# A fused attention and two-MLP kernel: the PSUM homes of the up and down products exchanged, and weight differences made early

## Chip, core and metric

The kernel runs on one core of a Trainium2 chip. The metric is the device time of one execution in microseconds (us); lower is better. Three runs of the kernel before are known.

## What is computed

Three stages follow each other on 2304 tokens (4 batches of 576), all in fp32:

```python
scores = scale * q @ k.T + (cum[:, None] - cum[None, :]), causal     # cum: cumsum of log f
x = softmax(scores) @ v                        # (2304, 512)
h = x @ w_in                                   # first MLP, 1024 wide
ln = layer_norm(h * softmax(h)) * g_ln
x = ln @ w_out                                 # (2304, 512)
h = maximum(x @ w2_in, 0)                      # second MLP, 2048 wide
out = (h * h) @ w2_out                         # (2304, 512)
```

## The kernel before

**Order of the work.** Every step (one instruction, or a few of one kind) is added to a plan with its costs per engine, a due time, the keys that it reads and writes, and the PSUM slot that it takes. The planner `Plan.lay` places all steps by list scheduling; the instructions are then issued in the order of the planned starts, so each engine and the DMA queue of SyncE (SP) works through a fixed list in that order. A step that gets more work or another due time moves its neighbours too. The planner knows PSUM by keys (`z0`, `z1`, `xo`, `h`, and slots of `pp` and `hp`). What an instruction really waits for is settled by the tile that it touches. `Z[0]`, `Z[1]`, `XO` and the three `PP` are tiles of one PSUM bank each; `HP` is one tile of two banks:

```python
    Z = [ps.tile([P, 512], F32, name=f"z{i}") for i in range(2)]
    HP = ps.tile([P, 2, 512], F32, name="hp")
    PP = [ps.tile([P, 512], F32, name=f"pp{i}") for i in range(3)]
```

**Arithmetic.** Each fp32 operand is split into a high and a low part (`halves`: a copy, line 345, 349 or 351, and a subtraction, line 1087); a product is three matmuls (low by high, high by low, high by high).

**Stages.** Attention and the first MLP run interleaved until about 480 us: scores in `z` (line 536), exp on ACT (571), transposes in `pp` (590), the product with v in `xo` (610), the first MLP's `h` in `hp` (826 to 828), its layer norm on all engines (the last scaling on POOL is line 887, the transposes that follow line 903), and `ln @ w_out` in `pp` (777 to 779). Meanwhile `early2` brings w2_in and w2_out, which arrive as words that need a conversion, through five slots of the tile `free` to DRAM; one addition on POOL for each piece is line 703. w2_out goes to `w2d` as it is. For w2_in also the differences and sums that are needed later are made here and stored in `w2u`, split into both halves.

**The second MLP** works on nine blocks of 256 tokens and eight pairs `p` of 128-row pieces of the 2048 wide hidden layer.

- `half_up` (line 1284) makes the hidden layer of block 0 for each pair with 24 matmuls; then ACT does relu in place (1248) and square to SBUF (1253). Pairs 0 and 1 use `pp`, pairs 2 to 7 the two banks of `hp`.
- `unit` (line 1334) makes it for two blocks at once for a pair, with seven products (of six matmuls) instead of eight; ACT and DVE add them up (lines 345, 1348), then relu and square (1248, 1366, 1253). Units with an even number use `hp`, odd ones two slots of `pp`.
- `step` (lines 1420 to 1422) makes the down product of one block and one pair, again seven products, each of three matmuls, in two groups of 9 and 12. DVE forms the operands (1392) and they are split. The products of a block add up over the eight pairs in `z0`, `z1`, `xo` and one slot of `pp` (`m7`); at the block's end a copy (345) and seven additions (1437) fold them into the output. The last block uses `hp` and `pp`.
- `weights2` loads the w2_out pieces of a pair from `w2d`, forms four differences on DVE (line 1151, 32 in all) and splits the results. `weightsh` does the like for the half step. Both go through six raw buffers.

Of the kernel before, what the change touches and what calls it, by code (L numbers as in the profile page):

```python
# [8 lines left out]
F32 = mybir.dt.float32  # L9
# [231 lines left out]
def tile_kernel(ctx: ExitStack, tc: tile.TileContext, q, k, v, f, w_in, w_out, g_ln, w2_in, w2_out, out):  # L241
# [6 lines left out]
    P = 128  # L248
# [25 lines left out]
    w2d = dram.tile([KF2, 2, P, 512], F32, name="w2d")  # L274
    w2u = dram.tile([KF2 // 2, 7, P, 512], F32, name="w2u")
    sb = ctx.enter_context(tc.tile_pool(name="sb", bufs=1))
# [52 lines left out]
    pl = Plan(dict(pp=3, hp=2, rq=NRQ), ("z0", "z1", "xo", "h"))  # L329
# [338 lines left out]
    def convert(src, raw, w, hi, lo, n, prio, rawk, wk, outk, gain=None, to=None):  # L668


        def words():
            dst = raw().bitcast(U32)
            if len(src.shape) == 3:
                dst = dst.rearrange("p (c x) -> p c x", x=src.shape[2])
            nc.sync.dma_start(dst, src)

        def L():
            return raw().rearrange("p (n t) -> p n t", t=2)[:, :, 0]

# [34 lines left out]
        pl.add(dict(pool=tt), a5, prio, [lk], [wk])  # L714
        if to is not None:
# [288 lines left out]
    small += GS[5:] + GA[6:]  # L1004
# [18 lines left out]
    def early2():  # L1023
# [12 lines left out]
        def unit(n, fc, c, hf, prio):  # L1036
            i = n % 5
            convert(
                source2(fc, 2 * c + hf), lambda: both(i), lambda: place(i, 2), None, None, 256,
                prio, ("fr", i), ("fw", i), ("w2d", fc, c, hf), to=w2d[fc, c, :, hf * 256 : hf * 256 + 256],  # L1040
            )
            return i

        def part2(i, p, k, prio):
# [9 lines left out]
            pl.add(dict(dma=1140), lambda: nc.sync.dma_start(w2u[p, k], both(i)), prio, [lk, hk], [("w2u", p, k)])  # L1054
# [7 lines left out]

        n = 0
        for fc in range(KF2):
            for hf in range(2):
                unit(n, fc, 1, hf, EARLY0 + n * EARLYP)
                n += 1
        for p in range(KP):
# [4 lines left out]
            for i, k in ((a11, 0), (a12, 4), (a22, 5)):  # L1073
                part2(i, p, k, prio)
# [4 lines left out]
            for i, k in ((a21, 2), (a22, 3), (a11, 1), (a12, 6)):  # L1079
                part2(i, p, k, prio)  # L1080
# [19 lines left out]
    def load2(fc, c, prio):  # L1100
        ri = turn[0] % len(RAW)
        turn[0] += 1
        once(("raw", ri), RAW[ri], rk2(ri), prio)
        pl.add(
            dict(dma=1140), lambda: nc.sync.dma_start(RAW[ri][0](), w2d[fc, c]), prio - AHEAD,
            [("w2d", fc, c, z) for z in (0, 1)], rk2(ri),
        )
        return ri
# [24 lines left out]
    def weights2(p, prio):  # L1133
        W = W2[p]
        rr = [load2(2 * p + i, 1, prio) for i in range(2)]

        def place(nm, n):
# [4 lines left out]
        def split(nm, raw, rk, n):  # L1142
            halves(raw, rk, W[nm + "h"][0], ("w2", p, nm + "h"), W[nm + "l"][0], ("w2", p, nm + "l"), n, prio)

        a, b = slice(0, 256), slice(256, 512)
        r = [[lambda i=i, z=z: RAW[rr[i]][0]()[:, z] for z in (a, b)] for i in range(2)]
        k = [rk2(rr[0]), rk2(rr[1])]

        def diff(dst, x, y, rk, wk):
            def fn():  # L1150
                nc.vector.tensor_tensor(out=dst(), in0=x(), in1=y(), op=ALU.subtract)

            pl.add(dict(dve=335), fn, prio, rk, wk, port=True)

        place("a", 256)
        place("b", 512)
        place("s", 512)
        place("t", 512)
# [66 lines left out]
    last8 = [("hp", "l0"), ("hp", "l1"), ("pp", "l2"), ("pp", "l3")]  # L1225

    def bank(blk, i):
        if blk == NTB - 1:
            return last8[(i + 1) // 2 if i == 6 else i // 2]
        return m7 if i == 6 else ("z0", "z1", "xo")[i // 2]  # L1230

    def psum(k):
        if k[0] == "hp":
            return HP[:, pl.slot[k]]
        if k[0] == "pp":
            return at(k)
        return Z[0] if k == "z0" else Z[1] if k == "z1" else XO.rearrange("p c x -> p (c x)")
# [32 lines left out]
    def half_up(p, prio):  # L1270
        uid[0] += 1
        ck = ("pp" if p < HPP else "hp", uid[0])
        if p == HPP:
            pl.add(dict(dve=0), lambda: None, prio - 5000, [], ["h", "hp"])
        W = H2[p]
        for y, c in ((0, 0), (0, 1), (1, 0), (1, 1)):
            def up(y=y, c=c):
# [10 lines left out]

            rk = [("w2", p, f"u{c}{a}") for a in "hl"] + [("xo", 5 + y, a) for a in range(2)] + ["hp"] * (p >= HPP)
            pl.add(  # L1290
                dict(pe=6 * 116), up, prio, rk, [ck] + ["turn"] * (y + c == 0), take=None if y + c else ck,
                uses=[ck] if y + c else [],
            )
# [6 lines left out]
    def unit(b, p, prio):  # L1300
        n = (b - 1) * KP + p
        pool = "pp" if n % 2 else "hp"
        uid[0] += 2
        ks = [(pool, uid[0] - 1), (pool, uid[0])]
        lastks[pool] = ks
# [12 lines left out]
        def prod(i, prio):  # L1318
            m = (7 * n + i) % NU
            sk = ("us", m)  # L1320
            if sk not in first_use:
                once(sk, again(upper[m]), [sk], prio)
            pl.add(
                dict(dma=1140), lambda: nc.sync.dma_start(upper[m][0]().bitcast(F32), w2u[p, i]), prio - UAHEAD,
# [3 lines left out]
            def fn():  # L1328
# [13 lines left out]
                dict(pe=6 * 116), fn, prio, [sk, ("xo", i, 0), ("xo", i, 1), "hp"], [k] + ["turn"] * (i == 0),  # L1342
                take=k if opens_ else None, uses=[] if opens_ else [k],
            )

        def add(dst, x, i, prio, rk, wk, uses=(), take=None):
# [4 lines left out]
            pl.add(dict(dve=344), fn, prio, [k] + rk, wk, uses=[k] + list(uses), take=take)  # L1351
# [3 lines left out]
        copy(TB, u2f, lambda: half(0), prio, [ks[0]], [uk], [ks[0]])  # L1355
# [6 lines left out]
        for i in (4, 5, 6):  # L1362
# [4 lines left out]
            uses=[k], take=r1,  # L1367
# [8 lines left out]
    def step(blk, p, prio):  # L1376
# [275 lines left out]
HPP = 2  # L1652
# [53 lines left out]
```

## Time and profile before

| what | value |
|---|---|
| median of 3 runs (lowest, highest) | 864.44 us (863.93, 867.23) |
| the profiled execution | 866.17 us |
| its span from the first to the last instruction | 864.4 us |
| PE busy | 805.0 us (93%) |
| weight loads of PE (PEld) busy | 729.0 us (84%) |
| DVE, ACT, POOL busy | 646.6, 543.2, 369.8 us |
| mean granted TensorE clock | 0.984 of full speed |
| DMA | 151.52 MB, 175 GB/s |

Matmuls are pipelined: a matmul of 256 columns is shown with some 0.28 us, while the next starts 0.12 us after it. So a busy PE is not PE at its peak. Idle time before an instruction is put down to the instruction that released it. A number on an instruction's line is the line of the kernel before.

### The profile page before, as it was taken

How to read it: one execution, taken by the hardware profiler on the slowest of the kernel's cores; microseconds unless marked ns; L12 is line 12 of the kernel's file. 1: busy time of each engine (PE TensorE's matmuls, PEld its weight loads, DVE VectorE, ACT ScalarE, POOL GpSimd, SP SyncE). 2: the span in 40 equal slices, each digit the busy share in tenths (PEclk: the TensorE clock that was granted, in tenths of full speed). 3: DMA queues.
4: the chain of work that ended last, by engine and by line, in shares of the span. 5: the costliest groups of instructions: out<-in, count | busy, mean ns of one | idle time of the engine just before them, and what ended most of it. 6: DMA issues, size and time to landing. Idle time of an engine off the chain costs nothing.

```text
span 864.4 us, 18663 instructions
## 1 busy us (share of the span) xinstructions
PE 805.0 (93%) x6392; PEld 729.0 (84%) x6392; DVE 646.6 (75%) x1655; ACT 543.2 (63%) x1383; POOL 369.8 (43%) x528
## 2 busy tenths in 40 slices
PE   4878899999999999999999888999999999999997
PEld 2556687888888888888989788999999999999997
DVE  8797867887767766866658769888678767876777
ACT  6899977988687887887857555454324433533332
POOL 6468767665587767687753010010111121112110
PEclk9999889999999999999999999999999999999999
DMA  6643336655555555645556666484757676665501
GB/s 208 191 146 116 115 94 205 199 175 171 166 165 177 177 154 167 208 160 166 177 191 205 190 205 243 154 279 144 241 178 237 188 229 205 198 207 172 158 1 49
DMA packets 99869, 151.52 MB, mean 175 GB/s; under 512 B 12128, under 2 KB 41824, under 8 KB 99776
## 3 DMA queue, kind: packets, MB, share of 16 engines
q1 hardware_dynamic: 99776, 150.35, 55.0%
q8 instruction: 50, 0.82, 0.4%
q14 instruction: 43, 0.35, 0.1%
HBM read 117.58 MB, written 32.65 MB: 174 GB/s over the span
## 4 chain that ended last, share of the span: by engine, by line
PE 73%; ACT 11%; DVE 11%; issue 3%; POOL 1%; DVEq 0%; ACTq 0%; POOLq 0%
PE hp L1334 9%; PE pp L1334 9%; PE pp L590 5%; PE z L536 5%; PE xo L610 4%; PE z L1420 3%; PE z L1421 3%; PE pp L777 3%; PE z L1422 3%; PE hp L826 3%; PE pp L779 3%; PE pp L778 3%; ACT adj L571 3%; PE hp L828 3%; PE hp L827 3%
## 5 line engine op out<-in xcount | busy, mean ns | idle before, releaser
L536 PE MATMUL z<-k,q 80*64 80x288 f32 (+17 forms) x384 | 95.8, 348 | 11.9 <-DVE q L501 8.2
L571 ACT ACTIVATE adj<-z,st 64x288 f32<-64x288 f32 (+9 forms) x192 | 95.3, 499 | 17.2 <-DVE st L557 15.2
L590 PE MATMUL pp<-ident,adj 128*128 128x128 f32 (+1 forms) x480 | 82.4, 282 | 16.9 <-ACT adj L571 15.2
L590 PEld LDWEIGHTS pp<-ident,adj 128*128 128x128 f32 (+1 forms) x480 | 52.8, 145 | 43.3 <-ACT adj L571 28.5
L557 DVE CUSTOM_DVE_ANT_0 z<-z,maskb 128x128 f32<-128x128 f32 (+8 forms) x144 | 65.4, 464 | 29.6 <-PE z L536 25.7
L777 PE MATMUL pp<-ln,woh 128*128 128x256 f32 x288 | 84.8, 294 | 2.2 <-DVE ln L906 1.5
L345 ACT COPY pt<-pp 128x256 f32<-128x256 f32 (+5 forms) x167 | 68.1, 418 | 24.3 <-PE pp L590 23.2
L779 PE MATMUL pp<-ln,woh 128*128 128x256 f32 x288 | 81.7, 284 | 0.0
L778 PE MATMUL pp<-ln,wol 128*128 128x256 f32 x288 | 81.7, 284 | 0.0
L1087 DVE TENSOR_TENSOR k<-adj,k 128x512 fp32r<-128x512 f32 x75 | 52.4, 700 | 38.2 <-POOL k L349 26.3
L349 POOL TENSOR_SCALAR k<-adj 128x512 fp32r<-128x512 f32 x39 | 24.2, 620 | 124.2 <-DVE adj L1392 50.7
L536 PEld LDWEIGHTS z<-k,q 128*128 128x128 f32 (+3 forms) x384 | 58.7, 189 | 20.0 <-ACT pt L1526 8.2
L703 POOL TENSOR_TENSOR free<-free 128x256 uint32<-128x256 uint32 x64 | 50.8, 799 | 47.5 <-DVE free L697 42.8
L610 PE MATMUL xo<-pt,vn 128*64 128x128 f32 (+1 forms) x960 | 64.9, 277 | 0.4 <-ACT pt L345 0.3
L826 PE MATMUL hp<-wih,xl 128*128 128x512 f32 x144 | 62.6, 435 | 1.1 <-ACT hp L865 1.1
L349 POOL TENSOR_SCALAR ln<-q 128x384 fp32r<-128x384 f32 x29 | 15.5, 534 | 111.6 <-PE z L1422 42.5
L610 PEld LDWEIGHTS xo<-pt,vn 128*64 128x64 f32 x960 | 51.5, 143 | 11.6 <-issue 6.8
L777 PEld LDWEIGHTS pp<-ln,woh 128*128 128x128 f32 x288 | 55.5, 193 | 4.8 <-DVE ln L906 2.0
L827 PE MATMUL hp<-wil,xh 128*128 128x512 f32 x144 | 57.5, 399 | 0.2 <-DVE wil L707 0.2
L828 PE MATMUL hp<-wih,xh 128*128 128x512 f32 x144 | 57.4, 399 | 0.0
L778 PEld LDWEIGHTS pp<-ln,wol 128*128 128x128 f32 x288 | 55.9, 194 | 0.6
L779 PEld LDWEIGHTS pp<-ln,woh 128*128 128x128 f32 x288 | 55.9, 194 | 0.0
(594 smaller groups left out, 2619.3 us busy)
## 6 DMA issues: line engine op xcount, KB each, us to landing
ln<-w2u SPq DMA_DIRECT2D x119, 256.0 KB
k<-w2u SPq DMA_DIRECT2D x105, 256.0 KB
w2u<-free SPq DMA_DIRECT2D x56, 256.0 KB
kn<-in_k_dram SPq DMA_DIRECT2D x32, 256.0 KB
free<-in_moe_w_out_dram SPq DMA_DIRECT2D x32, 256.0 KB
w2d<-free SPq DMA_DIRECT2D x64, 128.0 KB
free<-in_moe_w_in_dram SPq DMA_DIRECT2D x32, 256.0 KB
vn<-in_v_dram SPq DMA_DIRECT2D x20, 256.0 KB
```

The costliest lines, as they stand in the source:

```text
L345: nc.scalar.copy(dst(), src())
L536: nc.tensor.matmul(dst, lhsT=ql[0:r, p, 0:m], rhs=rhs, start=(g == 0), stop=(g == 1))
L571: nc.scalar.activation(out=adj[0:m, c[1] : c[2]], in_=Z[c[0]][0:m, 0 : c[2] - c[1]], func=AF.Exp, bias=st[0:m, low : low + 1], scale=-1.0, ...
L590: nc.tensor.transpose(at(sk)[:, (c - g) * m : (c - g + 1) * m], adj[0:m, zc : zc + P], ident[0:m, 0:m])
L610: nc.tensor.matmul(XO[own[j], g // 2, off : off + m], lhsT=VN[vslot[b, c]][:, (g + j) * D : (g + j + 1) * D], rhs=PT[(s - h + g + j) % NPT ...
L777: nc.tensor.matmul(px, lhsT=woh[:, fc, w], rhs=lo, start=(fc == 0), stop=False)
L778: nc.tensor.matmul(px, lhsT=wol[:, fc, w], rhs=hi, start=False, stop=False)
L779: nc.tensor.matmul(px, lhsT=woh[:, fc, w], rhs=hi, start=False, stop=(fc == KF - 1))
L826: nc.tensor.matmul(HP[:, c], lhsT=XL[i][:, cc, :], rhs=wih[:, cc, w], start=(cc == 0), stop=False)
L827: nc.tensor.matmul(HP[:, c], lhsT=XH[i][:, cc, :], rhs=wil[:, cc, w], start=False, stop=False)
L828: nc.tensor.matmul(HP[:, c], lhsT=XH[i][:, cc, :], rhs=wih[:, cc, w], start=False, stop=(cc == KC - 1))
L1334: nc.tensor.matmul(half(i), lhsT=l, rhs=r[:, x], start=(i in (0, 2) and c + k == 0), stop=(c + k == 3), skip_group_check=True,)
```

## The change

1. The products of `half_up` and of even units go to `z0` and `z1` instead of `hp` (pairs 0 and 1 of the half step too, which used `pp`); the down products that were in `z0` and `z1` go to the two banks of `hp` (keys `h0`, `h1`). In the last block they go to `z0`, `z1` and two slots of `pp`.
2. `early2` makes the differences of w2_out too and stores the seven pieces of each pair in `w2f`; for the last pair it stores both halves, in `w2s`. `weights2` loads them and only splits them; for the last pair it loads both halves to their places.
3. `XOP[0]`, the split token operand of the first product, moves from the space of w_out (`woh`) to that of the low layer norm (`ln1`); weights get the space in exchange. The planner's cost of a load becomes 900 from 1140.

```diff
-    w2d = dram.tile([KF2, 2, P, 512], F32, name="w2d")
+    w2d = dram.tile([KF2, P, 512], F32, name="w2d")
+    w2f = dram.tile([KF2 // 2 - NPRE, 7, P, 256], F32, name="w2f")
+    w2s = dram.tile([NPRE, 7, P, 512], F32, name="w2s")
...
-    c = carve("woh", [512] * 8)
-    large += c[:6]
-    XOP = c[6:] + carve("wol", [512] * 8) + [carve(f"vn{i}", [512])[0] for i in range(4)]
-    XOP = [XOP[2 * j : 2 * j + 2] for j in range(7)]
+    c = carve("woh", [512] * 7 + [256] * 2)
+    large += c[:7]
+    small += c[7:]
+    XOP = carve("wol", [512] * 8) + [carve(f"vn{i}", [512])[0] for i in range(4)]
+    XOP = [None] + [XOP[2 * j : 2 * j + 2] for j in range(6)]
...
-    GA = carve("ln1", [384] * 4 + [512] * 2 + [256] * 2)
+    GA = carve("ln1", [384] * 4 + [512] * 3)
     upper += GA[4:5]
-    large += GA[5:6]
+    XOP[0] = GA[5:7]
...
+        def keep(i, p, k, prio):
+            if p >= KP - NPRE:
+                part2(i, w2s[p + NPRE - KP, k], ("w2s", p, k), prio)
+            else:
+                pl.add(dict(dma=570), lambda: nc.sync.dma_start(w2f[p, k], place(i, 2)), prio, [("fw", i)], [("w2f", p, k)])
...
+            for i, k in ((r00, 0), (r10, 1), (r11, 2)):
+                keep(i, p, k, prio)
+            add2(r00, r01, r00, ALU.subtract, prio)
+            add2(r01, r11, r01, ALU.subtract, prio)
+            for i, k in ((r00, 3), (r01, 4)):
+                keep(i, p, k, prio)
+            add2(r11, r11, r00, ALU.subtract, prio)
+            add2(r10, r11, r10, ALU.subtract, prio)
+            for i, k in ((r10, 5), (r11, 6)):
+                keep(i, p, k, prio)
...
-        rr = [load2(2 * p + i, 1, prio) for i in range(2)]
...
-        split("a", r[0][0], k[0][0:1], 256)
-        diff(r[0][0], r[0][1], r[0][0], k[0][1:], k[0][0:1])
-        split("b", RAW[rr[1]][0], k[1], 512)
-        diff(r[0][1], r[1][1], r[0][1], k[1][1:], k[0][1:])
-        split("s", RAW[rr[0]][0], k[0], 512)
-        diff(r[1][1], r[1][1], r[0][0], k[0][0:1], k[1][1:])
-        diff(r[1][0], r[1][1], r[1][0], k[1][1:], k[1][0:1])
-        split("t", RAW[rr[1]][0], k[1], 512)
+        for nm, n in (("a", 256), ("b", 512), ("s", 512), ("t", 512)):
...
+            if p < KP - NPRE:
+                src = w2f[p, c[0]] if n == 256 else w2f[p, c[0] : c[0] + 2].rearrange("c p x -> p c x")
+                ri = load2(src, [("w2f", p, k) for k in c], n, prio)
+                halves(
...
-    last8 = [("hp", "l0"), ("hp", "l1"), ("pp", "l2"), ("pp", "l3")]
+    last8 = ["z0", "z1", ("pp", "l2"), ("pp", "l3")]
...
-        return m7 if i == 6 else ("z0", "z1", "xo")[i // 2]
+        return m7 if i == 6 else ("h0", "h1", "xo")[i // 2]
...
-        ck = ("pp" if p < HPP else "hp", uid[0])
+        ck = f"z{p % 2}"
...
-        pool = "pp" if n % 2 else "hp"
-        ks = [(pool, uid[0] - 1), (pool, uid[0])]
+        ks = [("pp", uid[0] - 1), ("pp", uid[0])] if n % 2 else ["z0", "z1"]
...
-HPP = 2
+NPRE, LOAD2 = 1, 900
```

How the order of the instructions moves, at three places. On PE in the half step, where a pair follows another (`hp`, or `z_120` and `z_121`, is the bank written; the second name is the weight; bracketed: the engines on which a row waits). Before:

```order
L1284 MATMUL hp<-vn_49_5089,k_49_5248 128x256 [waits Activation_49]
L1284 MATMUL hp<-vn_49_5041,k_49_5248 128x256 x2
L1284 MATMUL hp<-vn_49_5089,k_49_5248 128x256
L1284 MATMUL hp<-vn_49_5044,k_49_5248 128x256 [waits Activation_49]
L1284 MATMUL hp<-vn_49_4211,k_49_5248 128x256 x2
```

The change, at the beginning of a pair in `z1` and of the next in `z0`:

```order
L1300 MATMUL z_121<-vn_49_5106,k_49_5371 128x256 [waits Activation_49]
L1300 MATMUL z_121<-vn_49_5079,k_49_5371 128x256 [waits DVE_49]
L1300 MATMUL z_121<-vn_49_5079,k_49_5371 128x256 x2
L1300 MATMUL z_121<-vn_49_5074,k_49_5371 128x256
L1300 MATMUL z_120<-vn_49_5106,pt_5503 128x256 [waits Activation_49]
```

Before, a pair waits for ACT twice, after its 6th and its 12th matmul; in the change once, at its first, and the other wait is for the split of its weights.

On PE around the transposes of the last layer norm (`e` is its input), the end of the matmuls ahead of them and of those behind. Before:

```order
L1284 MATMUL hp<-vn_49_5041,wil_5221 128x256 x2
L903 MATMUL pp_123<-ident_99,e_90 128x128 x4
L903 MATMUL pp_124<-ident_99,e_90 128x128 x4
L1284 MATMUL hp<-vn_49_5089,k_49_5175 128x256
L777 MATMUL pp_123<-ln_49_668,woh_74 128x256
```

The change:

```order
L1300 MATMUL z_121<-vn_49_4494,wil_5257 128x256 x2
L907 MATMUL pp_126<-ident_101,e_92 128x128 x4
L907 MATMUL pp_125<-ident_101,e_92 128x128 x4
L1300 MATMUL z_120<-vn_49_5106,wil_5257 128x256
L781 MATMUL pp_126<-ln_49_670,woh_76 128x256
```

Between the last matmul of `x @ w_in` and these transposes stood 30 matmuls of `ln @ w_out` and 78 of the half step; now 42 and 48. Behind them 18 of the half step still come ahead of the last 96 of `ln @ w_out`.

On PE where the first down product begins. Before:

```order
L1334 MATMUL hp<-woh_5577,k_49_5097 128x256 x6
L1334 MATMUL hp<-wol_5589,k_49_5097 128x256 x18
L1334 MATMUL pp_124<-wol_5589,ln_49_5635 128x256 x12
L1420 MATMUL z_118<-free_5324,ln_49_5579 128x256
L1421 MATMUL z_118<-k_49_5097,ln_49_5579 128x256
```

The change:

```order
L1300 MATMUL z_121<-vn_49_4494,e_5570 128x256 x2
L1434 MATMUL hp<-free_5561,ln_49_5597 128x256
L1435 MATMUL hp<-woh_5573,ln_49_5597 128x256
L1434 MATMUL xo<-wih_5427,k_49_5022 128x256
L1346 MATMUL z_120<-ln_49_5597,k_49_5115 128x256 x6
```

Before, 66 matmuls of units stood between the half step and the first down product; now it follows at once, with 30 matmuls, and the units come behind. From the second block on, the two orders agree but for the names of the banks.

## Rows read from the trace of the kernel before

**Rows 1.** Windows: span, PE, PEld, DVE, ACT, POOL busy (instructions), clock, DMA share, GB/s.

```profile
120.00:455.00 335.00, 328.65 (x2667) 282.88 (x2666) 242.04 (x649) 266.37 (x761) 230.78 (x327) 0.99 0.56 175
...
482.00:512.00 30.00, 23.29 (x166) 21.49 (x166) 18.37 (x36) 13.76 (x29) 3.38 (x6) 0.94 0.54 169
512.00:864.40 352.40, 334.94 (x2790) 330.00 (x2788) 267.88 (x704) 140.23 (x284) 48.28 (x83) 1.00 0.57 182
```

**Rows 2.** Waits of PE from 455 us on: total us, times, longest.

```profile
PE hp L1334 <- DVE xw L1348: 3.5, 4, 1.0
PE hp L1334 <- ACT xw L345: 3.2, 6, 0.9
PE hp L1334 <- ACT q L1366: 3.2, 6, 0.7
PE hp L1284 <- ACT q L1253: 2.2, 3, 0.7
PE hp L1284 <- ACT hp L1248: 2.2, 3, 0.8
PE hp L1334 <- issue: 1.5, 1, 1.5
PE hp L1334 <- ACT adj L1366: 0.9, 2, 0.5
PE hp L1334 <- ACT xh L1366: 0.9, 2, 0.5
PE pp L1420 <- DVE k L1087: 0.7, 1, 0.7
PE z L1420 <- DVE ln L1087: 0.6, 1, 0.6
PE hp L1334 <- ACT qn L1366: 0.5, 1, 0.5
PE hp L1284 <- ACT adj L1253: 0.4, 1, 0.4
```

**Rows 3.** Timeline of PE, 470 to 530 us: start, us, instructions, idle before.

```profile
481.94 3.74 PE L1284 MATMUL hp<-vn,k 128*128 128x256 f32 x30
...
486.35 0.98 PE L1284 MATMUL hp<-vn,k 128*128 128x256 f32 x6 [0.67 <-ACT hp L1248]
...
488.07 1.69 PE L1284 MATMUL hp<-vn,k 128*128 128x256 f32 x12 [0.75 <-ACT q L1253]
...
489.60 0.88 PE L1284 MATMUL hp<-vn,pt 128*128 128x256 f32 x6
...
497.86 1.55 PE L1284 MATMUL hp<-vn,pt 128*128 128x256 f32 x6 [0.75 <-ACT q L1253]
```

**Rows 4.** Timeline of ACT, 481 to 512 us.

```profile
485.71 0.58 ACT L1248 ACTIVATE hp<-hp 128x512 f32<-128x512 f32 x1 [0.54 <-PE hp L1284]
487.42 0.60 ACT L1253 ACTIVATE q<-hp 128x512 f32<-128x512 f32 x1 [1.13 <-PE hp L1284]
```

**Rows 5.** Groups of PE by line from 440 us on: busy, mean ns, idle before.

```profile
L1334 PE MATMUL pp<-wol,ln 128*128 128x256 f32 x234 | 31.1, 279 | 0.0
```

**Rows 6.** Timelines of PE and POOL around the last layer norm.

```profile
454.27 0.40 PE L828 MATMUL hp<-wih,xh 128*128 128x512 f32 x1
...
464.24 1.84 POOL L887 TENSOR_SCALAR e<-e,sm 128x1024 f32<-128x1024 f32 x1
...
467.32 1.04 PE L903 MATMUL pp<-ident,e 128*128 128x128 f32 x8
```

**Rows 7.** Timelines of DVE and PE at the end of block 0.

```profile
556.93 0.75 DVE L1437 TENSOR_TENSOR kn<-x,z 128x256 f32<-128x256 f32 x2
...
557.96 0.28 PE L1420 MATMUL z<-free,ln 128*128 128x256 f32 x1
```

**Rows 8.** Lines L703 and L1151: ns of one (least/median/most), first and last start.

```profile
L703 POOL TENSOR_TENSOR free<-free x64: 727/746/1200, 104.6 to 432.9; 128x256 uint32<-128x256 uint32 x64
...
L1151 DVE TENSOR_TENSOR kn<-kn x8: 419/426/717, 464.7 to 528.3; 128x256 f32<-128x256 f32 x8
```

More of the change, by code (lines that the diff above doesn't have):

```diff
@@ L328, in tile_kernel @@
     NU, NRQ = 13, 11
-    pl = Plan(dict(pp=3, hp=2, rq=NRQ), ("z0", "z1", "xo", "h"))
+    pl = Plan(dict(pp=3, hp=2, rq=NRQ), ("z0", "z1", "xo", "h", "h0", "h1"))
     uid = [0]
@@ L714, in convert @@
         pl.add(dict(pool=tt), a5, prio, [lk], [wk])
+        if to is False:
+            return
         if to is not None:
@@ L983, in tile_kernel @@
     more("free", 7, 1)
-    c = carve("woh", [512] * 8)
-    large += c[:6]
-    XOP = c[6:] + carve("wol", [512] * 8) + [carve(f"vn{i}", [512])[0] for i in range(4)]
-    XOP = [XOP[2 * j : 2 * j + 2] for j in range(7)]
-    more("k10", 5, 1, upper)
+    c = carve("woh", [512] * 7 + [256] * 2)
[3 more added lines that the diff above has]
+    XOP = [None] + [XOP[2 * j : 2 * j + 2] for j in range(6)]
+    upper += carve("k10", [512] * 5)
     GS = carve("k11", [512] * 5 + [256])
     upper += GS[4:5] + carve("ln0", [512] * 6)
-    GA = carve("ln1", [384] * 4 + [512] * 2 + [256] * 2)
+    GA = carve("ln1", [384] * 4 + [512] * 3)
     upper += GA[4:5]
-    large += GA[5:6]
+    XOP[0] = GA[5:7]
     at_h = len(large)
@@ L1003, in tile_kernel @@
     more("xc", 0, 3)
-    small += GS[5:] + GA[6:]
+    small += GS[5:]
     RQ = [carve(a, [512], F32)[0] for a in ["qn", "xh0", "adj2"] + [f"q1{i}{j}" for i in range(2) for j in range(2)]]
@@ L1039, in unit, with part2 @@
                 source2(fc, 2 * c + hf), lambda: both(i), lambda: place(i, 2), None, None, 256,
-                prio, ("fr", i), ("fw", i), ("w2d", fc, c, hf), to=w2d[fc, c, :, hf * 256 : hf * 256 + 256],
+                prio, ("fr", i), ("fw", i), ("w2d", fc, hf), to=False if c else w2d[fc, :, hf * 256 : hf * 256 + 256],
             )
             return i
-        def part2(i, p, k, prio):
+        def part2(i, dst, key, prio):
             hi, lo = (lambda: place(i, 0).bitcast(F32R)), (lambda: place(i, 1).bitcast(F32R))
@@ L1053, in part2 @@
             s = pl.add(dict(dve=335, pool=686), sub, prio, [w, lk], [hk], port=True)
-            pl.add(dict(dma=1140), lambda: nc.sync.dma_start(w2u[p, k], both(i)), prio, [lk, hk], [("w2u", p, k)])
+            pl.add(dict(dma=1140), lambda: nc.sync.dma_start(dst, both(i)), prio, [lk, hk], [key])
         def add2(i, x, y, op, prio):
@@ L1061, in add2 @@
             s = pl.add(dict(dve=335, pool=686), fn, prio, [("fw", x), ("fw", y)], [("fw", i)], port=True)
-        n = 0
[L1064 to L1067, printed above, removed]
+        def keep(i, p, k, prio):
[3 more added lines that the diff above has]
+                pl.add(dict(dma=570), lambda: nc.sync.dma_start(w2f[p, k], place(i, 2)), prio, [("fw", i)], [("w2f", p, k)])
+        n = 0
+        for p in range(KP):
+            prio = EARLY0 + 4 * p * EARLYP
+            r00, r01, r10, r11 = (
+                unit(n + 2 * a + hf, 2 * p + a, 1, hf, prio + EARLYP * (2 * a + hf)) for a in range(2) for hf in range(2)
+            )
+            n += 4
+            prio += 4 * EARLYP
+            for i, k in ((r00, 0), (r10, 1), (r11, 2)):
[8 more added lines that the diff above has]
+                keep(i, p, k, prio)
         for p in range(KP):
@@ L1073, in early2 @@
             for i, k in ((a11, 0), (a12, 4), (a22, 5)):
-                part2(i, p, k, prio)
+                part2(i, w2u[p, k], ("w2u", p, k), prio)
             add2(a22, a22, a21, ALU.add, prio)
@@ L1079, in early2 @@
             for i, k in ((a21, 2), (a22, 3), (a11, 1), (a12, 6)):
-                part2(i, p, k, prio)
+                part2(i, w2u[p, k], ("w2u", p, k), prio)
     def halves(raw, rk, hi, hk, lo, lk, n, prio, uses=()):
@@ L1098, in tile_kernel, with load2 @@
     turn = [0]
-    def load2(fc, c, prio):
+    def load2(src, rk, n, prio):
         ri = turn[0] % len(RAW)
@@ L1103, in load2, with fn @@
         once(("raw", ri), RAW[ri], rk2(ri), prio)
[L1104 to L1107, printed above, removed]
+        def fn():
+            dst = RAW[ri][0]()[:, 0:n]
+            nc.sync.dma_start(dst.rearrange("p (c x) -> p c x", x=256) if len(src.shape) == 3 else dst, src)
+        pl.add(dict(dma=LOAD2 * n / 512), fn, prio - AHEAD, rk, rk2(ri)[0 : n // 256])
         return ri
@@ L1115, in weightsh @@
         for c in range(2):
-            ri = load2(2 * p + c, 0, prio)
+            ri = load2(w2d[2 * p + c], [("w2d", 2 * p + c, z) for z in range(2)], 512, prio)
             for a in "hl":
@@ L1134, in weights2 @@
         W = W2[p]
-        rr = [load2(2 * p + i, 1, prio) for i in range(2)]
-        def place(nm, n):
+        o = 0
+        for nm, n in (("a", 256), ("b", 512), ("s", 512), ("t", 512)):
+            c = range(o, o + n // 256)
+            o += n // 256
             for a in "hl":
@@ L1140, in place, with fn @@
                 claim(W[nm + a], [("w2", p, nm + a)], prio)
[L1142 to L1158, printed above, removed]
-        split("a", r[0][0], k[0][0:1], 256)
-        diff(r[0][0], r[0][1], r[0][0], k[0][1:], k[0][0:1])
-        split("b", RAW[rr[1]][0], k[1], 512)
-        diff(r[0][1], r[1][1], r[0][1], k[1][1:], k[0][1:])
-        split("s", RAW[rr[0]][0], k[0], 512)
-        diff(r[1][1], r[1][1], r[0][0], k[0][0:1], k[1][1:])
-        diff(r[1][0], r[1][1], r[1][0], k[1][1:], k[1][0:1])
-        split("t", RAW[rr[1]][0], k[1], 512)
+            if p < KP - NPRE:
+                src = w2f[p, c[0]] if n == 256 else w2f[p, c[0] : c[0] + 2].rearrange("c p x -> p c x")
+                ri = load2(src, [("w2f", p, k) for k in c], n, prio)
+                halves(
+                    lambda ri=ri, n=n: RAW[ri][0]()[:, 0:n], rk2(ri)[0 : n // 256], W[nm + "h"][0], ("w2", p, nm + "h"),
+                    W[nm + "l"][0], ("w2", p, nm + "l"), n, prio,
+                )
+                continue
+            for y, a in enumerate("hl"):
+                def fn(dst=W[nm + a][0], c=c, n=n, y=y):
+                    src = w2s[p + NPRE - KP, c[0] : c[0] + n // 256, :, y * 256 : y * 256 + 256]
+                    nc.sync.dma_start(
+                        dst().bitcast(F32).rearrange("p (c x) -> p c x", x=256), src.rearrange("c p x -> p c x")
+                    )
+                pl.add(
+                    dict(dma=LOAD2 * n / 512), fn, prio - AHEAD, [("w2s", p, k) for k in c], [("w2", p, nm + a)]
+                )
     def xload(ri, g, tok, prio):
@@ L1229, in bank @@
             return last8[(i + 1) // 2 if i == 6 else i // 2]
-        return m7 if i == 6 else ("z0", "z1", "xo")[i // 2]
+        return m7 if i == 6 else ("h0", "h1", "xo")[i // 2]
     def psum(k):
[L1233 to L1237, printed above, removed]
+        if k in ("h0", "h1"):
+            return HP[:, int(k[1])]
+        if k in ("z0", "z1"):
+            return Z[int(k[1])]
+        return XO.rearrange("p c x -> p (c x)") if k == "xo" else at(k)
     def acc(blk, i):
@@ L1270, in half_up @@
     def half_up(p, prio):
-        uid[0] += 1
-        ck = ("pp" if p < HPP else "hp", uid[0])
-        if p == HPP:
-            pl.add(dict(dve=0), lambda: None, prio - 5000, [], ["h", "hp"])
+        ck = f"z{p % 2}"
         W = H2[p]
@@ L1287, in up @@
                         )
[L1289 to L1293, printed above, removed]
+            rk = [("w2", p, f"u{c}{a}") for a in "hl"] + [("xo", 5 + y, a) for a in range(2)]
+            pl.add(dict(pe=6 * 116), up, prio, rk, [ck] + ["turn"] * (y + c == 0))
         r = new_r(0, p, prio)
-        relu(lambda: psum(ck), lambda: psum(ck), 512, prio, [], [ck], [ck], True)
-        square(rof(0, p), lambda: psum(ck), 512, prio, [ck, "rqs"], [r], [ck], True, take=r)
+        relu(lambda: psum(ck), lambda: psum(ck), 512, prio, [], [ck], [], True)
+        square(rof(0, p), lambda: psum(ck), 512, prio, [ck, "rqs"], [r], [], True, take=r)
     uprods = [(0, 0), (0, 1), (1, 0), (1, 1), (0, 0), (1, 0), (1, 1)]
@@ L1301, in unit @@
         n = (b - 1) * KP + p
-        pool = "pp" if n % 2 else "hp"
         uid[0] += 2
-        ks = [(pool, uid[0] - 1), (pool, uid[0])]
-        lastks[pool] = ks
+        ks = [("pp", uid[0] - 1), ("pp", uid[0])] if n % 2 else ["z0", "z1"]
+        lastks[n % 2] = ks
         s1, s2 = (2 * b - 1, p), (2 * b, p)
@@ L1323, in prod @@
             pl.add(
-                dict(dma=1140), lambda: nc.sync.dma_start(upper[m][0]().bitcast(F32), w2u[p, i]), prio - UAHEAD,
+                dict(dma=LOAD2), lambda: nc.sync.dma_start(upper[m][0]().bitcast(F32), w2u[p, i]), prio - UAHEAD,
                 [("w2u", p, i)], [sk],
@@ L1341, in prod @@
             pl.add(
-                dict(pe=6 * 116), fn, prio, [sk, ("xo", i, 0), ("xo", i, 1), "hp"], [k] + ["turn"] * (i == 0),
-                take=k if opens_ else None, uses=[] if opens_ else [k],
+                dict(pe=6 * 116), fn, prio, [sk, ("xo", i, 0), ("xo", i, 1)], [k] + ["turn"] * (i == 0),
+                take=k if opens_ and n % 2 else None, uses=slots_of([] if opens_ else [k]),
             )
@@ L1350, in add @@
             k = ks[uprods[i][0]]
-            pl.add(dict(dve=344), fn, prio, [k] + rk, wk, uses=[k] + list(uses), take=take)
+            pl.add(dict(dve=344), fn, prio, [k] + rk, wk, uses=slots_of([k]) + list(uses), take=take)
         for i in range(4):
             prod(i, prio)
-        copy(TB, u2f, lambda: half(0), prio, [ks[0]], [uk], [ks[0]])
+        copy(TB, u2f, lambda: half(0), prio, [ks[0]], [uk], slots_of([ks[0]]))
         add(u2f, u2f, 1, prio, [], [uk])
@@ L1366, in unit @@
             dict(act=264), lambda: nc.scalar.activation(out=c11(), in_=half(0), func=AF.Relu), prio, [k, "rqs"], [r1],
-            uses=[k], take=r1,
+            uses=slots_of([k]), take=r1,
         )
@@ L1408, in step @@
         if p == 0 and blk in (0, NTB - 1):
-            for k in [m7] if blk == 0 else last8:
-                pl.add(dict(pe=0), lambda: None, prio + DOWN, lastks[k[0]] if blk else [], [k], take=k)
+            for k in [m7] if blk == 0 else last8[2:]:
+                pl.add(dict(pe=0), lambda: None, prio + DOWN, lastks[1] if blk else [], [k], take=k)
+            if blk == 0:
+                pl.add(dict(pe=0), lambda: None, prio, [], ["h", "h0", "h1"])
         end = blk == NTB - 1 and p == KP - 1
```

## Prediction

> **What bounds the kernel now.** I read the windows first, then PE's waits, then the timeline at the waits. In the attention stage PE idles 335.00 - 328.65 = 6.35 us [rows 1]: there is little to win. From 482 to 512 us it idles 6.7 of 30 us, and the clock falls to 0.94; from 512 us on 17.5 us are idle, 4.5 of them the output at the end. DVE is busy 61% and 76% of these two windows, DMA 54% and 57%: PE is the nearest to full, and what it waits for counts. The waits of PE from 455 us on are a list of twelve [rows 2]. Nine of them, 28 waits, name hp and are released by ACT or DVE; no unit of pp stands there, though half the units use pp: 234 of their matmuls show 0.0 us of idle [rows 5].
>
> Why hp waits is in the timeline. PE issues 30 matmuls (24 of one pair, 6 of the next, which goes to the other bank), then idles until ACT's relu; 6 more, then idles until ACT's square [rows 3]. The relu starts at 485.71, after the 30, though its own pair had ended 6 matmuls sooner, and the square waits 1.13 us for PE again [rows 4]. The two banks of hp are one tile, so a reader of one bank waits for the writer of the other, and the other way round. Engines that should overlap take turns.
>
> **The change, part by part.**
>
> *Up products in z0, z1.* These are two tiles, as the slots of pp are. Waits that go: in the half step 2.2 + 2.2 + 0.4 = 4.8 us in 7; in the units 3.5 + 3.2 + 3.2 + 0.9 + 0.9 + 0.5 = 12.2 us in 21 [rows 2]. A wait costs more than its idle: 30 matmuls in 3.74 us, the last shown 0.28 long, are (3.74 - 0.28) / 29 = 0.119 us each, so the next group was due at 481.94 + 30 x 0.119 = 485.51. It starts at 486.35, that is 0.84 late where 0.67 idle is shown, and lasts 0.98 where six without a wait last 0.88 [rows 3]: 0.27 on top. 28 x 0.27 = 7.6 us. With the waits the clock goes too: granted 0.94 in 482 to 512, so 0.06 x 30 = 1.8 us; six matmuls at 497.86 last 1.55 us, near the lower of the two levels (1.2 instead of 2.4 GHz), after 16 us of stopping and starting [rows 1, 3]. Together **26.4 us**. That z then waits for nothing of its own I take from pp [rows 5]; a bound from the other side is that half of the units' waits stay: (12.2 + 21 x 0.27) / 2 = 8.9 us less.
>
> *Down products in hp.* They are written for a whole block and read at its end only, so the turn-taking can cost there alone. The copy of the first product now also waits for the second group's writes to the other bank. The last two folds end at 557.68, and the next block's first matmul starts at 557.96 [rows 7]: 0.28 us of slack. The group of 12 writes hp in its 7th to 9th matmul, so the copy can slip by at most 9 x 0.119 = 1.1 us, a wait of at most 0.8 + 0.27 at each of 7 ends: 0 to 7.5 us. ACT takes the copy late anyway between its relus, so I stay near zero: 0.2 each, **1.4 us**.
>
> *Last transposes.* From the last matmul of x @ w_in (454.27) to the end of the scaling on POOL (464.24 + 1.84 = 466.08) are 11.8 us; the transposes come at 467.32 behind 108 matmuls [rows 6]. Now 90 are ahead of them, 90 x 0.119 = 10.7 us. PE waits some 1.1: **1.4 us** with the restart (0 to 3).
>
> *Weights.* The late part loses 32 differences of 0.42 us [rows 8], 13.4 us of DVE, and four splits. They are beside PE's work and save nothing by themselves. But the first down product comes 66 matmuls sooner in the order, 7.9 us, and the stalls ahead of it go, so its weights are due some 15 us sooner. The loads grow too: seven pieces for four, 4 MB more. At the rate of 169 GB/s for a share of 0.54 [rows 1] that is 13 us of all DMA engines, in about 55 us that have some 45% free. DVE idles 11.6 us in 482 to 512 [rows 1] and gets its 13.4 back, so most of the 15 us is there: **2 us** (0 to 8).
>
> *Early part.* In the attention stage POOL gets 39 additions of 0.75 us [rows 8], 29 us, and loses 15 copies; SP issues 24 stores more. POOL is busy 230.8 of 335 us there, PE idles 6.35 [rows 1]. The pieces lie in five slots of their own, on which PE does not wait in this stage: **0** (from 2 us gained to another 6.35 lost, a doubling of PE's idle).
>
> The Trainium skill (SBUF — State Buffer, section Who interferes with whom) speaks against this part: VectorE with two SBUF inputs and GpSimd exclude each other, and whoever comes second waits for the other's whole instruction. The row agrees only in its extreme: of 64 such additions the middle one takes 746 ns against 727 at least, and one 1200 [rows 8]; whether DVE is held up it does not tell. By the rule an estimate is 29 us x 0.72 (DVE's share) = 21 us more on DVE, and were PE to wait for all of it, the sum would be about 864.
>
> *Sum*, against the profiled execution: 866.17 - 26.4 + 1.4 + 1.4 + 2 = 844.6. The median of the runs is 1.7 us below that execution, so **843 us**.
>
> **The rivals.**
>
> *The weights become the bound* (0.12). PE, faster, meets splits that are not done between 482 and 530 us. For it: the sooner first down product, and SP's list, where a load that waits for a raw buffer holds up those behind. Against it: DVE's idle. If half of the 15 us is missing, 7.5 + 843 = 851.
>
> *The exchange moves the turn-taking to the block ends* (0.05): all 7 ends pay 1.07 instead of 0.2, 6.1 us more: 849. Against it is the late copy.
>
> *The change doesn't do what it says* (0.05): z0 and z1 are single homes, so that a unit waits for the reads of the one before it, and half the units' waits stay: 852. Against it: two slots of pp do as much with no idle.
>
> *Slower* (0.04): the 39 additions stand in POOL's list ahead of what attention needs of POOL (the keys' low parts, the layer norm's scaling), and all 29.1 us reach PE: 843 + 29 = 872. It decides from the point where 21.6 us, the net gain, reach PE: 29 of the 39 additions. Against it: POOL idles 104 us in that stage.
>
> **How the numbers follow.** My forecast has 0.74. Its best end: nothing is given back and the three waits that stay (1.5 + 0.7 + 0.6 us [rows 2] and 3 x 0.27) go too: 864.44 - 26.4 - 3.6 = 834. Its worst: all upper bounds, 3 + 7.5 + 8 + 6.35 = 24.9: 863. Both ends at once are unlikely; 836 to 857 leaves out the slower rival and the worst tail, and holds the first three rivals. A measurement here tells about 0.5%, 4.3 us, from no change. Faster by more: nearly all of the forecast and of the first three rivals, 0.90. Within: 0.06. Slower by more: 0.04.
>
> **What would show it.** Right: no wait of PE on z in the half step and at most a few in the units; waits from 455 us on below 8 us instead of 17 on hp alone; a clock of 1.00 from 482 us on; the first down product before 496 us. The attention stage's windows unchanged within 3 us. Wrong: waits on DVE's splits (line 1111 of the changed kernel) in the first block, a gap ahead of each block's first down product, or the last x @ w_in more than 5 us later than at 454.27.

## Result and profile after

The changed kernel takes 840.08 us (median of 4 runs, 836.60 to 842.38) against 864.18 us (861.42 to 867.23) in runs on the same chip: a ratio of 0.972, 95% interval [0.967, 0.976]. A second set of runs gave 839.88 against 864.94 us, 0.971 [0.968, 0.974]. The profiled execution took 840.62 us, its span is 838.8 us; PE is busy 791.1 us (94%), DMA moves 159.66 MB (190 GB/s), the mean clock is 0.986.

The same windows as in [rows 1], and the one from 455 to 482 us (span; PE, PEld, DVE, ACT, POOL busy with their instructions; clock, DMA share, GB/s), of the changed kernel. Line numbers in this part and in the experiments are those of each run's own kernel; in the changed kernel 1300 is a product of the half step, 1346 of a unit, 1434 of a down product, 347 and 1111 the two halves of a split:

```profile
120.00:455.00 335.00, 328.90 (x2669) 283.00 (x2669) 241.58 (x648) 280.12 (x803) 247.48 (x334) 1.00 0.59 185
455.00:482.00 27.00, 25.62 (x219) 25.22 (x218) 18.91 (x33) 16.93 (x38) 10.49 (x13) 1.00 0.80 233
482.00:512.00 30.00, 26.91 (x216) 26.56 (x215) 24.44 (x49) 20.14 (x40) 2.89 (x5) 0.94 0.90 294
512.00:838.80 326.80, 320.26 (x2705) 319.24 (x2703) 251.84 (x662) 127.80 (x259) 50.96 (x87) 1.00 0.62 197
```

From 482 to 512 us PE runs 216 matmuls where it ran 166 [rows 1]. The DMA share is 0.90 there, against 0.54. (A window's share counts the whole time of the packets that begin in it, so it can pass 1.) In the attention stage PE is as before, but ACT is busy 13.8 us longer and POOL 16.7 us.

All waits of PE from 440 us on, to be laid beside [rows 2] (engine, what it wrote, line, what released it: total us, times, longest):

```profile
PE pp L1346 <- ACT k L347: 2.6, 1, 2.6
PE z L1300 <- ACT adj L1272: 0.9, 1, 0.9
PE xo L1434 <- DVE k L1111: 0.8, 2, 0.5
PE pp L1434 <- DVE k L1111: 0.7, 1, 0.7
PE pp L1346 <- DMA ln<-w2u: 0.5, 1, 0.5
PE z L1300 <- ACT q L1272: 0.5, 1, 0.5
PE z L1346 <- DVE q L1360: 0.3, 1, 0.3
```

The 28 waits on hp are gone. Three short ones on z stand in their place (0.9, 0.5 and 0.3 us). Before, the list had 31 waits and 19.8 us [rows 2], now 8 and 6.3 us. With 0.27 us of restart for each, the prediction's figure, that is 28.2 less 8.5 = 19.7 us. The stretch from the start of the last x @ w_in (at 447.12 us, before at 454.27 [rows 6]) to the end of the span went from 410.1 to 391.7 us, 18.4 us less, and it now holds 16 matmuls more, 1.9 us: 20.3. The waits explain it; the clock does not, since it is 0.94 from 482 to 512 us before [rows 1] and after.

New is one wait of a unit in `pp`, where there was none [rows 5]. PE's timeline there (start, us, instructions, idle before):

```profile
503.68 0.86 PE L1346 MATMUL pp<-wol,ln 128*128 128x256 f32 x6
507.11 0.94 PE L1346 MATMUL pp<-wol,ln 128*128 128x256 f32 x6 [2.56 <-ACT k L347]
508.58 1.62 PE L1346 MATMUL pp<-vn,ln 128*128 128x256 f32 x6 [0.53 <-DMA ln<-w2u]
```

The last six last 1.62 us where six at full clock last 0.86, near the lower of the clock's two levels (1.2 instead of 2.4 GHz). The profile names ACT for the 2.56 us. A second profile of the same kernel has for this place

```profile
508.18 0.95 PE L1346 MATMUL pp<-wol,ln 128*128 128x256 f32 x6 [2.98 <-DMA ln<-w2u]
```

so I read it as a load of w2_in's pieces that is late; the copy that the first profile names (`k`, a split of w2_out's pieces) is nothing that this matmul reads. In the second profile the clock stays at 1.00 there, which I had not expected:

```profile
482.00:512.00 30.00, 26.86 (x226) 26.48 (x225) 24.91 (x50) 20.78 (x42) 3.70 (x5) 1.00 0.93 298
```

For the matmul at 508.58 the chain of waits of the first profile says why (start, us, what):

```profile
501.56 0.43 DVE maskb L1360
501.99 0.26 SPq L1131
502.25 0.05 issue
502.30 0.46 SPq L1336
502.76 0.05 issue
502.81 5.63 DMA ln<-w2u
508.44 0.14 issue
508.58 1.62 PE pp L1346 x6
```

SP's list has a load of w2_out's pieces (line 1131) ahead, which waits for DVE; behind it two loads of w2_in's pieces (line 1336) start, and the second takes 5.63 us. Around it, in windows of 10 us:

```profile
500.00:510.00 10.00, 6.91 (x52) 6.56 (x50) 9.18 (x21) 6.53 (x13) 1.51 (x2) 0.90 0.93 306
510.00:520.00 10.00, 9.70 (x76) 9.50 (x76) 7.40 (x21) 5.09 (x12) 0.62 (x1) 0.93 1.08 368
520.00:530.00 10.00, 9.51 (x81) 9.30 (x80) 8.13 (x23) 5.00 (x10) 0.62 (x1) 1.00 0.97 340
```

By these shares the DMA engines are full here, at 306 to 368 GB/s. Before, the window from 500 to 510 us had 0.47 and 158 GB/s.

### The profile page after: what moved, and what is told of

Same layout as the page of the kernel before. It is cut to its first block, busy times and chain, and to the rows that moved or that the text cites. A ratio compares the mean times of both kernels' runs of the same rounds, so it can differ in the third digit from the quotient of the medians.

```text
span 838.8 us, 18711 instructions
## 1 busy us (share of the span) xinstructions
PE 791.1 (94%) x6392; PEld 720.3 (86%) x6392; DVE 632.9 (75%) x1614; ACT 550.6 (66%) x1414; POOL 393.5 (47%) x544
## 2 busy tenths in 40 slices
DMA packets 109663, 159.66 MB, mean 190 GB/s; under 512 B 12832, under 2 KB 52768, under 8 KB 109568
## 4 chain that ended last, share of the span: by engine, by line
PE 69%; ACT 13%; DVE 8%; DMA 4%; issue 3%; POOL 3%; SPq 0%; DVEq 0%; POOLq 0%; ACTq 0%
PE z L1346 9%; PE pp L1346 9%; PE pp L592 5%; PE xo L612 4%; PE z L538 4%; PE hp L1434 3%; PE hp L1436 3%; PE hp L1435 3%; PE hp L830 3%; ACT adj L573 3%; PE hp L832 3%; PE hp L831 3%; PE pp L781 2%; PE pp L782 2%; PE pp L783 2%
## 5 line engine op out<-in xcount | busy, mean ns | idle before, releaser
L538 PE MATMUL z<-k,q 80*64 80x288 f32 (+17 forms) x384 | 93.6, 344 | 9.0 <-DVE q L503 8.2
L781 PE MATMUL pp<-ln,woh 128*128 128x256 f32 x288 | 83.6, 290 | 1.5 <-DVE ln L910 1.5
L347 ACT COPY pt<-pp 128x256 f32<-128x256 f32 (+5 forms) x170 | 69.2, 420 | 18.1 <-PE pp L592 16.7
L783 PE MATMUL pp<-ln,woh 128*128 128x256 f32 x288 | 80.6, 280 | 0.0
L612 PE MATMUL xo<-pt,vn 128*64 128x128 f32 (+1 forms) x960 | 63.2, 271 | 0.7 <-ACT pt L347 0.3
L781 PEld LDWEIGHTS pp<-ln,woh 128*128 128x128 f32 x288 | 54.8, 190 | 4.5 <-DVE ln L910 1.8
L783 PEld LDWEIGHTS pp<-ln,woh 128*128 128x128 f32 x288 | 54.5, 189 | 0.0
```

What stands on the lines that cost most here:

```text
L347: nc.scalar.copy(dst(), src())
L538: nc.tensor.matmul(dst, lhsT=ql[0:r, p, 0:m], rhs=rhs, start=(g == 0), stop=(g == 1))
L612: nc.tensor.matmul(XO[own[j], g // 2, off : off + m], lhsT=VN[vslot[b, c]][:, (g + j) * D : (g + j + 1) * D], rhs=PT[(s - h + g + j) % NPT ...
L781: nc.tensor.matmul(px, lhsT=woh[:, fc, w], rhs=lo, start=(fc == 0), stop=False)
L783: nc.tensor.matmul(px, lhsT=woh[:, fc, w], rhs=hi, start=False, stop=(fc == KF - 1))
```

## The experiments

The theory (T): the gain comes from the two banks of hp being one tile. Rivals: it comes from the early differences and the sooner first down product (R), or from the banks themselves (S). The later runs ask what the other parts of the change cost. Times are medians of 4 to 10 runs, ratios are against the kernel before on the same chip.

| run | us | ratio, 95% interval |
|---|---|---|
| hp as two tiles | 837.88, again 838.49 | 0.969 [0.966, 0.972], 0.970 [0.968, 0.972] |
| part 1 alone | 839.52 | 0.970 [0.968, 0.973] |
| parts 2, 3 alone | 863.99 | 0.998 [0.997, 1.000] |
| the change, z0 and z1 one tile | 909.30 | 1.051 [1.049, 1.054] |
| hp as two tiles, parts 2, 3 | 839.25 | 0.971 [0.969, 0.973] |
| the change, four pieces of a pair loaded instead of seven | 838.31 | 0.969 [0.967, 0.971] |
| the change, planned load cost 1140 | 849.80 | 0.983 [0.981, 0.985] |
| hp as two tiles, planned load cost 900 | 836.92 | 0.968 [0.966, 0.970] |
| the change, w2_in's loads 20 us ahead | 837.16 | 0.968 [0.965, 0.971] |
| hp as two tiles, parts 2, 3, 20 us ahead | 836.93 | 0.970 [0.967, 0.973] |

### Two tiles at the same place

```diff
-    HP = ps.tile([P, 2, 512], F32, name="hp")
+    ph = tc.tile_pool(name="ph", bufs=1, space=PSUM)
+    HP = ph.__enter__().tile([P, 2, 512], F32, name="hp")
+    HB = []
+    def hbank(i):
+        if not HB:
+            ph.__exit__(None, None, None)
+            p2 = ctx.enter_context(tc.tile_pool(name="p2", bufs=1, space=PSUM))
+            HB.extend(p2.tile([P, 512], F32, name=f"hb{j}") for j in range(2))
+        return HB[i]
...
-            return HP[:, pl.slot[k]]
+            return hbank(pl.slot[k])
```

> The kernel before with one edit: after the last h has been read, hp's two banks become two tiles of one bank each, at the same place; the order on every engine stays the same. Theory T (the change gains because the two banks of one tile make PE and its readers take turns): the 28 waits on hp go, 17.0 us of idle and 7.6 us of restarts, and the time is 838 to 848 us. Rival R (it gains because the differences are made early and the first down product comes sooner): 861 to 866 us. Rival S (PE needs other banks, not other tiles: readers and writers of the same two banks would wait in any case): the waits stay under the new names, 861 to 866 us.

837.88 us: T, at the lower end of its range. All waits of PE from 455 us on, then the timelines of PE in the half step and of ACT at a relu and its square, against [rows 2, 3, 4]:

```profile
PE hb L1343 <- DVE adj L1357: 1.4, 1, 1.4
PE z L1429 <- DVE ln L1096: 0.7, 1, 0.7
PE pp L1429 <- DVE k L1096: 0.7, 1, 0.7
PE xo L1429 <- DVE k L1096: 0.3, 1, 0.3
```

```profile
479.63 5.91 PE L1293 MATMUL hb<-vn,k 128*128 128x256 f32 x48
485.37 3.76 PE L1293 MATMUL hb<-vn,pt 128*128 128x256 f32 x30
```

```profile
482.69 0.58 ACT L1257 ACTIVATE hb<-hb 128x512 f32<-128x512 f32 x1 [0.46 <-PE hb L1293]
483.30 0.60 ACT L1262 ACTIVATE q<-hb 128x512 f32<-128x512 f32 x1
```

PE issues 48 and 30 matmuls without a stop, and the square follows the relu at once, where it waited 1.13 us [rows 4]. Nothing else in the program differs: every engine runs the same instructions in the same order. The two slots are still two banks side by side, but hp is made behind `pp` in this kernel, so that they need not be the same banks as before; the trace has no addresses. That the waits are the tile's and not the banks' is settled further down, by the run with z as one tile. From the start of the last x @ w_in (452.65 us) to the end are 384.0 us, before 410.1: 26.1 us less. The clock does not fall in this stretch (1.00 from 482 to 512 us). A second set of runs:

> The kernel with hp in two tiles once more, beside the runs of this call: 836 to 840 us, and no wait of PE on a load. It is the base for the run with parts 2 and 3 on top.

838.49 us, and again no wait on a load; its stretch is 384.1 us.

### The parts of the change alone

Part 1 alone is the change without `w2f`, `w2s`, the move of `XOP[0]` and the planned cost of 900; parts 2 and 3 alone are these three with all products in their old homes.

> Part 1 of the change alone: up products in z0 and z1, down products in hp's banks; w_out's differences stay in the late part, with four loads for a pair. T: 838 to 848 us, no wait on z in the half step by readers of the other bank, and up to 8 us of waits for the splits of weights, as DVE has its 13.4 us of differences still to do. R: 858 to 866 us.

> Parts 2 and 3 of the change alone: differences made early, XOP[0] moved, cost of a load 900; all products keep their homes. T: the 28 waits on hp stay (17 us of idle), 858 to 866 us. R: 838 to 846 us.

839.52 and 863.99 us: T both times, and R falls. With parts 2 and 3 alone all 28 waits on hp stay, 17.4 us, with a load beside them (all waits of PE from 455 us on, the first four of 12):

```profile
PE pp L1353 <- DMA ln<-w2u: 3.3, 1, 3.3
PE hp L1303 <- ACT hp L1267: 3.2, 3, 1.5
PE hp L1353 <- DVE xw L1367: 2.9, 3, 1.0
PE hp L1353 <- ACT xw L347: 2.8, 6, 0.5
```

### The other way round: z as one tile

```diff
-    Z = [ps.tile([P, 512], F32, name=f"z{i}") for i in range(2)]
+    ZZ = ps.tile([P, 2, 512], F32, name="z")
+    Z = [ZZ[:, i] for i in range(2)]
```

> The changed kernel with z0 and z1 as the two banks of one tile; nothing else is edited. Attention's scores use z too, so the stages are read apart. T: from 455 us on some 28 waits on z come back, 17 us of idle and 7.6 us of restarts, 858 to 866 us from that alone, and attention loses more (its scores take turns with ACT's exp): over 866 us in all. R: from 455 us on waits stay under 8 us.

909.30 us: T. The banks, the instructions and their order are those of the change, and the turns come back wherever z is used: from 455 us on the products of the half step and of the units wait 34 times on z, 22.0 us, where T had said some 28 and 17. So S falls too. The three largest of PE's waits from 455 us on, then the two largest of the attention stage (120 to 487 us), and last the only wait on z of that stage in the change (120 to 447 us):

```profile
PE z L1301 <- ACT z L1268: 4.4, 6, 0.8
PE z L1347 <- ACT q L1379: 3.7, 6, 1.4
PE z L1301 <- ACT q L1273: 3.3, 4, 1.0
```

```profile
PE z L539 <- ACT adj L574: 7.4, 18, 0.8
PE z L539 <- DVE st L560: 3.3, 12, 0.5
```

```profile
PE z L538 <- ACT adj L573: 0.4, 1, 0.4
```

The last x @ w_in starts at 487.08 us, 38 to 40 us later than in the two profiles of the change (447.12, 449.52), and what follows it takes 419.9 us, 28 to 32 more. Two edits of the tile alone move the time down by 26 to 28 us and up by 69 (from the change's 839.88 on another chip; the ratios are 1.051 and 0.971).

### What the early differences are worth

> Parts 2 and 3 of the change on top of the kernel with hp in two tiles. If these parts are worth something once the waits on hp are gone (DVE relieved of 32 differences): 830 to 835 us. If they only add traffic: a wait of PE on a load of w2_in's pieces near 500 us (3.3 us in the run of parts 2 and 3 alone, 2.6 us in the change), a fall of the clock behind it, and 838 to 845 us.

839.25 us beside 838.49: nothing, and the wait on a load is there (2.8 us), with a clock of 0.87 and 0.96 in the windows from 500 to 510 and to 520 us.

In the next run a load brings one piece instead of two, `nc.sync.dma_start(dst[:, 0:256], src[:, 0])`; the other half of the raw buffer keeps old words.

> The changed kernel, but the loads of two pieces of w_out's differences bring only the first piece, so that a pair loads the 512 KB that it loaded before; the second pieces hold old words, the order and the planned costs stay. If the traffic causes the wait of 2.6 us at 507 us: no wait there, DMA share below 0.9 from 500 to 530 us, clock 1.00, and 834 to 838 us. If the order of SP's list causes it (loads for units behind loads that wait for raw buffers): the wait stays, over 2 us.

838.31 us, just above the first range. The wait shrinks from 2.6 to 0.6 us and the clock stays at 1.00; a new wait of 1.2 us on a split of the weights takes part of it back. The DMA share from 500 to 510 us is 0.82, but behind that 1.02 and 1.04: below 0.9 it was not, as I had expected.

> The changed kernel with the loads of w2_in's pieces planned 20 us ahead of their due time instead of 14. If the wait of 2.6 us at 507 us is these loads standing too late in SP's list: it goes, and the time is 835 to 838 us, if nothing else comes late. If the DMA engines are full there (share 0.93 to 1.08 from 500 to 530 us), something else waits instead: 838 to 845 us.

The edit is `UAHEAD`, 20000 for 14000. 837.16 us, as the first expectation said, and the wait is gone with all the traffic there. The seven loads of that unit went out until 503.2 us in the change, here until 496.3 (SP's timeline, the last of them), and PE does not stop from 500 to 510 us (window):

```profile
495.79 0.47 SPq L1336 DMA_DIRECT2D ln<-w2u  x1
```

```profile
500.00:510.00 10.00, 10.00 (x87) 10.00 (x87) 9.10 (x21) 7.02 (x16) 1.72 (x3) 1.00 0.95 318
```

So full DMA engines alone do not stop PE. The loads of w2_in's pieces stood too late in SP's list for the 5.63 us that a load took there. Less traffic or an earlier place both cure it.

### The planned cost of a load

> The changed kernel with the planned cost of a load back at 1140. If the order that the planner makes causes the wait at 507 us: it goes or moves, 834 to 838 us. If the traffic causes it: a wait of 2 us or more on a load stays between 490 and 520 us, 838 to 842 us.

> The kernel with hp in two tiles, the planned cost of its late loads (w_out's pieces and w2_in's) at 900 instead of 1140. If this cost is good by itself: 834 to 837 us. If it only suits the seven loads of the change: 837 to 842 us, with a wait on splits or loads between 480 and 530 us.

849.80 us with 1140: no expectation held. The waits on loads are down to 0.5 us, but the splits come late instead, and the clock falls twice (0.83 from 510 to 520 us, 0.83 from 575 to 595 us). The three largest of PE's waits from 440 us on:

```profile
PE hp L1434 <- DVE ln L1111: 2.4, 2, 1.4
PE z L1346 <- DVE xw L1360: 2.3, 1, 2.3
PE hp L1435 <- DVE k L1111: 2.2, 1, 2.2
```

With seven loads for a pair the planned cost decides 10 us. With four loads it decides little: 836.92 us with 900, beside 837.88 and 838.49 with 1140, and no wait above 1.3 us. That lies in the first range, but a gain of 1 to 1.6 us is within the scatter.

### All together

> The kernel with hp in two tiles, parts 2 and 3 of the change on top, and the loads of w2_in's pieces planned 20 us ahead: as the run before with parts 2 and 3 (839.25 us), less its wait of 2.8 us and the fall of the clock behind it. If that wait is all that these parts cost, and the relief of DVE is worth something: 833 to 836 us. If the relief of DVE is worth nothing: 836 to 839 us.

836.93 us, the same as without parts 2 and 3 and with the planned cost of 900 (836.92): the relief of DVE is worth nothing. These three kernels near 837 us have the lowest medians of the study. The change's two sets (836.35 to 842.09 in the second, 839.88) lie 3 us above them; the sets overlap, and no ratio between them was measured.

## Why the prediction was right

The forecast was 843 us, the chip says 840, inside the range of 836 to 857. The mechanism is the one forecast; that the number came so near is in part luck, since the small terms were wrong in both directions.

- **Waits on hp, 26.4 us: right.** Measured alone, by two tiles, it is 26.1 us of the profile's tail and 26 to 28 us of the median (864.75 to 838.49; 865.96 to 837.88). Also right was that a wait costs more than its idle: the idle alone was 17.0 us. The clock of 1.00 from 482 us on was wrong for the change's first profile (0.94), where another wait came; in its second (1.00) and with two tiles alone it held. That z waits for nothing of its own was not quite so: 0.9 and 0.5 us in the half step, 0.3 us in a unit.
- **Block ends, 1.4 us: not paid.** No wait on hp is released by a fold in the change. At the end of block 0 the last two folds and the next block's first product are

```profile
540.10 0.75 DVE L1451 TENSOR_TENSOR kn<-x,hp 128x256 f32<-128x256 f32 x2
```

```profile
543.34 0.28 PE L1434 MATMUL hp<-free,ln 128*128 128x256 f32 x1
```

  2.5 us of slack instead of 0.28 [rows 7]. Part 1 alone is 1 to 1.6 us above two tiles in place, within the scatter. With the planned cost of 1140 one end did pay: a product into hp waits 1.0 us for a fold.
- **Last transposes, 1.4 us: not paid** here: the transposes have no idle before them, since the scaling on POOL ended 10.2 us after the start of the last x @ w_in, at 457.31 us, and not 11.8 as before; it took 1.20 us instead of 1.84 [rows 6].

```profile
456.11 1.20 POOL L891 TENSOR_SCALAR e<-e,sm 128x1024 f32<-128x1024 f32 x1
```

```profile
458.38 1.04 PE L907 MATMUL pp<-ident,e 128*128 128x128 f32 x8
```

  With part 1 alone PE did wait 0.8 us for POOL there.
- **Weights, 2 us (0 to 8): the size about right by luck, the reason wrong.** I expected late splits; these cost 1.5 us in three waits, and before it was 1.3 us in two [rows 2]. What came late was a load of w2_in's pieces, which my step did not name: 3.1 us of idle, and a fall of the clock. Put right, it gave 2.7 us back (839.88 to 837.16; the two sets overlap). My estimate took 13 us of extra traffic against a mean of 45% free over 55 us. The 10 us windows read 0.93, 1.08 and 0.97, and the loads of the units lie in SP's list among those of the weights.
- **Early part, 0 us (-2 to 6.35): a gain of about 2 us.** In eight profiles with part 2 (z as one tile left out) the last x @ w_in starts at 446.0 to 449.8 us (mean 448.1), in four profiles without it and with the order before at 451.2 to 454.3 (452.5). Of the 4.3 us, 16 matmuls that now stand behind it are 1.9. Why the remaining 2.4 us are gained was not tried. The medians show no gain, since the stretch behind it is longer: 388.0 us with parts 2 and 3 on two tiles, 384.1 without, and only 1.9 of that are the 16 matmuls.
- The Trainium skill's rule against this part (SBUF — State Buffer, section Who interferes with whom) is not borne out as a cost. POOL is busy 16.7 us longer from 120 to 455 us, and DVE 241.58 us as against 242.04 [rows 1].
- **A step that I left out: the planned cost of a load.** I wrote of it in no term. Part 2 without it is 849.8 us, which is near the rival "the weights become the bound" (851), and in part by its mechanism: 4.1 us of PE's waits are on splits between 501 and 523 us, another 4.3 us came from 580 to 593 us.
- **The signs.** Held: 6.3 us of waits, below 8; the first down product at 489.30 us, before 496; PE's share of the attention stage. Not held: no wait on z in the half step, the clock in the first profile, and the attention windows of ACT and POOL, which moved by more than 3 us.

The sum of 844.6 stands 4.0 us above the profiled execution. In this profile 5.2 us are gained up to the last x @ w_in, where I took nothing (7.15 us sooner, less 1.9 for the 16 matmuls). Behind it the waits with their restarts and the fall of the clock, 8.5 + 1.8 us, make 10.3, where my terms left 3.6 + 1.4 + 1.4 + 2 = 8.4. That is 3.3 of the 4.0 us; the rest is open.

The gain, then, is the whole of part 1, and of part 1 only that two banks written and read by turns stand in two tiles. Parts 2 and 3 bring nothing that shows.

## What to carry to other kernels

A PSUM tile of two banks, used as two slots, makes the writer of one slot wait for the reader of the other. Look in the waits for a name whose slots alternate and whose waits another pair of slots does not show, and give each slot a tile of its own. Before a change that moves work from an engine to loads, read the DMA share in 10 us windows at the place where the loads go, and which other loads stand behind them in the queue's list.

## What the runs showed of the hardware

- PE wrote one bank while ACT read the other, without a stop, once the two were two tiles (48 matmuls in 5.91 us, with a relu and a square inside them). The Trainium skill (PSUM — Partial Sum Buffer, section PSUM bank collisions raise a hardware error) asks for guards by bank and quadrant, or more simply by bank. The runs agree that a guard by bank is enough here: the one over two banks cost 26 us. No run here left a bank without a guard.
- The clock does not fall after every such wait. A wait of 2.56 us at 507 us was followed by the lower level (a granted clock of 0.90 and 0.93 in the windows from 500 to 520 us), one of 2.98 us at the same place in the second profile of the same kernel was not (1.00).
- The DMA engines moved 368 GB/s over 10 us at a share of 1.08 in the change. At 318 GB/s and 0.95 PE did not stop when the loads were issued earlier, where at 306 GB/s and 0.93 it had waited 3.1 us for loads issued later.
